# Second MLP layer as seven half-block products, interleaved with quarters of the next step's first layer

## The chip, the cores and the metric

One core of a Trainium2 chip runs the program. The metric is device time in microseconds of one launch; the time before is the median of three runs. A profiled execution of the same program gives the trace from which single instructions are read. Engines are named as in the profile: PE is TensorE (matmuls, with PEld for its weight loads), DVE is VectorE, ACT is ScalarE, POOL is GpSimd, SP is the queue that issues the DMAs.

## What is computed

A spectral block followed by an MLP, each with a layer norm ahead of it and a residual. The input has 2048 rows of 576 elements, the MLP has 4608 hidden elements, all in float32.

```python
def _A_ref(x, w_r, w_i):
    B, S, D = x.shape
    X = jnp.fft.rfft2(x, axes=(-2, -1))
    X = X * (w_r + 1j * w_i)
    return jnp.fft.irfft2(X, s=(S, D), axes=(-2, -1))

def _B_ref(x, w1, w2):
    h = jnp.einsum("bsd,df->bsf", x, w1)
    h = jnp.maximum(h, 0)
    return jnp.einsum("bsf,fd->bsd", h, w2)

h = x + _A_ref(_layernorm(x), A_w_r, A_w_i)
h2 = h + _B_ref(_layernorm(h), B_w1, B_w2)
```

The change lies in the MLP's second product, relu(h) times w2.

## The kernel before

The spectral block is done by matrix products with constant DFT matrices. Its inverse part runs in a loop over 16 row tiles and hands the normalised, transposed rows to the MLP (`project`) in four chunks `xc[c]` of 512 rows. The residual stays in `xs`, 16 tiles of 128 rows by 576, to which every partial result of the MLP is added.

The MLP is cut into 18 groups `g` of 256 hidden elements and 4 chunks `c` of 512 rows, so there are 72 steps, listed in `steps`: the first eight in an order of their own, partly woven into the inverse part, then group by group. The engines take their work in the order in which the code writes it (a manual schedule); the program sets the semaphores.

To get float32 accuracy out of the faster fp32r matmuls, every operand is held as a rounded part and a remainder (`h` and `l`), and each product is three matmuls: h by h, h by l, l by h. ACT writes the rounded part and DVE subtracts it from the original for the remainder. `split_weights` does this for a group's weights, part 0 for w1 and part 1 for w2 (L313).

A step has two halves. `mm1(i, a)` computes 128 hidden elements of a chunk (a is 0 or 1) as 14 matmuls with 512 columns into half of a PSUM tile of two banks; after the second half ACT takes the relu (L464) and DVE the remainder (L465). `mm2(i, tt)` multiplies one row tile of the chunk with the group's w2 in 12 matmuls of 288 columns, and DVE adds the PSUM tile to `xs` (L482). A step has four `mm2`. In the last loop, step i + 1's two `mm1` stand ahead of step i's four `mm2`, so that the relu runs beside matmuls that don't need it. The next group's weights are loaded five steps ahead and split three steps ahead. GpSimd (POOL) has no work in this loop. PSUM tiles come from a ring of four, and SBUF tiles of the tag "e" from ten buffers. In the last group each finished chunk of `xs` (in the last chunk: each finished tile) is stored by two DMAs.

Of the kernel before, what the change touches and what calls it, by code (L numbers as in the profile page):

```python
# [126 lines left out]
def kernel(ctx: ExitStack, tc: tile.TileContext, x, w_r, w_i, w1, w2, cc2, c1, fb, ib, c3, out):  # L127
    nc = tc.nc
# [15 lines left out]

    def mm(o, l, r, start, stop):
        nc.tensor.matmul(o, l, r, start=start, stop=stop)  # L146

    def act(o, i, **kw):
        nc.scalar.activation(o, i, AF.Copy, **kw)  # L149
# [142 lines left out]
    raw, wts = {}, {}  # L292

    def load_weights(g):
        v1, v2 = ebuf([128, 5, 256]), ebuf([128, 2, D])
        f = slice(256 * g, 256 * g + 256)
        nc.sync.dma_start(v1[:, 0:4], w1[0:512, f].rearrange("(a p) f -> p a f", p=128))
        for h in range(2):
            nc.sync.dma_start(v1[64 * h:64 * h + 64, 4], w1[512:576, f])
        nc.sync.dma_start(v2, w2[f, :].rearrange("(a p) d -> p a d", p=128))  # L300
        raw[g] = (v1, v2)

    def split_weights(g, part, eng):
        if g not in wts:
            if g % 2:
                w = tail[0][:, 4608:]
                w = (w[:, 0:1280], w[:, 1280:2560], w[:, 2560:3712], w[:, 3712:4864])
            else:
                w = (ebuf([128, 1280], F32R), ebuf([128, 1280], F32R), ebuf([128, 1152], F32R), ebuf([128, 1152], F32R))
            wts[g] = [v.rearrange("p (a n) -> p a n", a=a) for v, a in zip(w, (5, 5, 2, 2))]  # L310
        h, l = wts[g][2 * part:2 * part + 2]
        act(h, raw[g][part])
        eng.tensor_sub(l, raw[g][part], h)  # L313
# [63 lines left out]
    xs = sb([128, NT, D], "A")  # L377
# [7 lines left out]
    xc = [xc01[:, 0], xc01[:, 1], xc2]  # L385
    Es = {}

    def inv_d(t):
        pd = ps()
        ut = [dims(U, 64 * (32 * b + 2 * t), [1, 128]) for b in range(5)]  # L390
        for r in range(2):
            o = pd[:, 512 * r:512 * r + 290]
            mm(o, ut[4], lpv[:, r], True, False)
            for h in range(2):
                mm(o[:, 145 * h:145 * h + 145], ut[2 * ((r + h) % 2) + r], dev[:, 2 * r + h], False, h == 1)
        ez = ebuf([128, 578 + D])
# [7 lines left out]
        nc.vector.tensor_add(ea, ea, pb_)  # L404
        y = ez[:, 578:]
        nc.gpsimd.tensor_sub(dims(ez, 578 + 575, [-1, 287]), e0[:, 1:288], e1[:, 1:288])
        nc.vector.tensor_add(y[:, 0:289], e0, e1)  # L407
# [37 lines left out]
    hid = {}  # L445
    pend = {}

    def mm1(i, a):
        g, c = steps[i]
        w1h, w1l = wts[g][:2]  # L450
        if a == 0:
            pend[i] = ps()
        p = pend[i][:, 512 * a:512 * a + 512]
        f = slice(128 * a, 128 * a + 128)
        ops = []
        for kt in range(4):
            ops += [(w1h, kt, kt), (w1h, kt, 5 + kt), (w1l, kt, kt)]
        ops += [(w1h, 4, 4), (w1l, 4, 4)]
        for n_, (w, kt, xk) in enumerate(ops):
            mm(p, w[:, kt, f], xc[c][:, xk, :], n_ == 0, n_ == len(ops) - 1)  # L460
        if a == GF - 1:
            p = pend.pop(i).rearrange("p (a s) -> p a s", a=GF)
            hh, hl = sb([128, GF, 512], "D", 4, F32R), sb([128, GF, 512], "D", 4, F32R)
            nc.scalar.activation(hh, p, AF.Relu)  # L464
            nc.vector.scalar_tensor_tensor(hl, p, 0.0, hh, op0=ALU.max, op1=ALU.subtract)  # L465
            hid[i] = (hh, hl)
# [2 lines left out]

    def mm2(i, tt):  # L470
        g, c = steps[i]
        w2h, w2l = wts[g][2:]
# [9 lines left out]
        nc.vector.tensor_add(xt, xt, pv)  # L482
        if tt == CH - 1:
            seen[c] += 1
            hid.pop(i)
        if g == NG - 1 and (c == NC - 1 or tt == CH - 1):
            a = t if c == NC - 1 else CH * c
            for j in range(2):
                nc.sync.dma_start(ov[j, :, a:t + 1, :], xs[64 * j:64 * j + 64, a:t + 1, :])
# [71 lines left out]
```

## Time and profile before

| | |
|---|---|
| Time, median of 3 runs (lowest to highest) | 1108.53 us (1108.38 to 1109.08) |
| Profiled execution: its time | 1108.31 us |
| Profiled execution: span of its instructions | 1106.5 us |
| Granted TensorE clock, mean | 0.999 |
| HBM read, written | 42.23 MB, 4.72 MB |
| DVE additions to `xs` (L482): count, busy | 288, 216.4 us |
| Hidden relu on ACT (L464): count, busy | 72, 73.9 us |
| Relu remainder on DVE (L465): count, busy | 72, 88.2 us |

A row of the groups reads: line, engine, operation, tile written and tiles read by the program's names (buffer numbers left out), shapes, count, then the busy time in us and the mean duration of one in ns, then the engine's idle time just before them and what ended it. A row of the timeline reads: start in us from the start of the span, length in us, engine, line, operation, tiles, count, and in brackets the idle time before it. In the names, d is PSUM, D holds the hidden rows, X, B and C the normalised input chunks (X also split weights), e the small buffers, A is `xs`.

### The profile page before, as it was taken

To read this page: it belongs to the slowest core of one execution; us is meant where nothing else is said; L and a number is where in the kernel's file an instruction comes from. 1 tells how busy PE (TensorE), PEld (TensorE's weight loads), DVE (VectorE), ACT (ScalarE), POOL (GpSimd) and SP (SyncE) were. 2 spreads that over 40 slices of the span, in tenths; PEclk is the share of its full clock that TensorE was granted. 3 is DMA by queue.
4 is the path that set the end of the run, shared out by engine and by line. 5 is a ranking of instruction groups with operands and counts; after the bars stand their busy time and mean duration, and the time that the engine had idled before them with its cause. 6 is when DMAs were issued, how large, how long until landed. Compare 5 with 4: busy or idle time off the path is not lost.

```text
span 1106.5 us, 15686 instructions
## 1 busy us (share of the span) xinstructions
PE 1089.2 (98%) x6944; PEld 975.4 (88%) x6944; DVE 483.1 (44%) x739; ACT 199.3 (18%) x238; POOL 67.5 (6%) x116
## 2 busy tenths in 40 slices
PE   8999999999999999999999999999999999999997
PEld 7787778899899998989999899999889999998997
DVE  7577776434334343334343333434233434333333
ACT  4533253510101010101101011101010110101100
POOL 4200264300000000000000000000000000000000
PEclk9999999999999999999999999999999999999999
DMA  8922601111011001100200110011003001000015
GB/s 232 260 58 73 146 1 46 47 46 46 1 46 46 1 1 55 37 1 5 86 1 1 46 46 1 1 46 46 1 1 91 1 1 46 1 1 1 1 44 129
DMA packets 27573, 47.97 MB, mean 43 GB/s; under 512 B 2673, under 2 KB 18289, under 8 KB 27121
## 3 DMA queue, kind: packets, MB, share of 16 engines
q1 hardware_dynamic: 27504, 46.96, 15.6%
q8 instruction: 55, 0.90, 0.3%
q14 instruction: 14, 0.11, 0.0%
HBM read 42.23 MB, written 4.72 MB: 42 GB/s over the span
## 4 chain that ended last, share of the span: by engine, by line
PE 95%; DVE 3%; ACT 1%; issue 0%; POOL 0%; DMA 0%; SPq 0%; DVEq 0%; ACTq 0%; POOLq 0%
PE d L146 94%; PE d L434 1%; DVE st L206 0%; DVE A L416 0%; ACT e L220 0%; DMA X<-in_A_x_dram 0%; DVE e L313 0%; DVE e L404 0%; DVE e L403 0%; POOL r L210 0%; DVE e L407 0%; DVE e L348 0%; DVE e L250 0%; DVE e L347 0%; PE d L435 0%
## 5 line engine op out<-in xcount | busy, mean ns | idle before, releaser
L482 DVE TENSOR_TENSOR A<-A,d 128x576 f32<-128x576 f32 x288 | 216.4, 752 | 135.0 <-PE d L146 134.8
L465 DVE SCALAR_TENSOR_TENSOR D<-d,D 128x1024 fp32r<-128x1024 f32 x72 | 88.2, 1225 | 422.3 <-ACT D L464 422.3
L146 PEld LDWEIGHTS d<-e,D 128*128 128x128 f32 x1728 | 233.0, 188 | 3.9 <-DVE D L465 0.6
L146 PE MATMUL d<-e,D 128*128 128x288 f32 x1728 | 236.0, 295 | 0.3 <-DVE D L465 0.3
L146 PEld LDWEIGHTS d<-X,D 128*128 128x128 f32 x1728 | 232.2, 188 | 2.9
L146 PE MATMUL d<-X,D 128*128 128x288 f32 x1728 | 234.0, 294 | 0.0
L464 ACT ACTIVATE D<-d 128x1024 fp32r<-128x1024 f32 x72 | 73.9, 1027 | 767.4 <-PE d L146 767.4
L146 PE MATMUL d<-B,e 128*128 128x512 f32 x504 | 120.8, 395 | 0.4 <-DVE A L416 0.4
L146 PE MATMUL d<-B,X 128*128 128x512 f32 x504 | 119.0, 392 | 0.0
L146 PEld LDWEIGHTS d<-B,e 128*128 128x128 f32 x504 | 93.7, 188 | 21.6 <-ACT e L149 0.8
L146 PEld LDWEIGHTS d<-B,X 128*128 128x128 f32 x504 | 93.6, 188 | 19.4
L146 PE MATMUL d<-C,e 128*128 128x512 f32 x252 | 60.2, 395 | 0.0
L146 PE MATMUL d<-X,e 128*128 128x512 f32 x252 | 60.0, 394 | 0.0
L146 PE MATMUL d<-C,X 128*128 128x512 f32 x252 | 59.1, 391 | 0.0
L146 PE MATMUL d<-X 128*128 128x512 f32 x252 | 58.8, 390 | 0.0
L146 PEld LDWEIGHTS d<-X,e 128*128 128x128 f32 x252 | 46.8, 188 | 10.4
L146 PEld LDWEIGHTS d<-C,e 128*128 128x128 f32 x252 | 46.8, 188 | 10.3
L146 PEld LDWEIGHTS d<-C,X 128*128 128x128 f32 x252 | 46.8, 188 | 9.6
L146 PEld LDWEIGHTS d<-X 128*128 128x128 f32 x252 | 46.8, 188 | 9.3
L146 PE MATMUL d<-cc,e 128*128 128x256 f32 (+1 forms) x160 | 32.9, 361 | 3.0 <-DVE e L252 2.7
L146 PE MATMUL d<-e,A 128*64 128x145 f32 (+1 forms) x384 | 34.1, 327 | 0.8 <-ACT A L149 0.8
L146 PEld LDWEIGHTS d<-cc,e 128*128 128x128 f32 x160 | 28.5, 190 | 7.3 <-issue 2.9
(64 smaller groups left out, 629.3 us busy)
## 6 DMA issues: line engine op xcount, KB each, us to landing
e<-in_B_w_dram SPq DMA_DIRECT2D x18, 576.0 KB, 5.1
e<-in_B_w_dram SPq DMA_DIRECT2D x18, 512.0 KB, 3.7
A<-in_A_x_dram SPq DMA_DIRECT2D x16, 288.0 KB, 8.5
X<-in_A_x_dram SPq DMA_DIRECT2D x12, 288.0 KB, 7.4
out_dram<-A SPq DMA_DIRECT2D x6, 576.0 KB, 5.5
e<-in_B_w_dram SPq DMA_DIRECT2D x36, 64.0 KB, 3.6
B<-in_A_w_r_dram SPq DMA_DIRECT2D x15, 144.5 KB, 6.9
B<-in_A_w_i_dram SPq DMA_DIRECT2D x15, 144.5 KB, 7.0
```

The source lines that it names most:

```text
L146: nc.tensor.matmul(o, l, r, start=start, stop=stop)
L434: nc.tensor.transpose(pz[:, 128 * b:128 * b + 128], y[:, 128 * b:128 * b + 128], ident)
L464: nc.scalar.activation(hh, p, AF.Relu)
L465: nc.vector.scalar_tensor_tensor(hl, p, 0.0, hh, op0=ALU.max, op1=ALU.subtract)
L482: nc.vector.tensor_add(xt, xt, pv)
```

## The change

From step 8 on, the second layer of a step is computed by Strassen's scheme in Winograd's form. The hidden block is cut into four blocks: A11 and A21 are the two 256-row halves of the first 128 hidden elements, A12 and A22 those of the second. The group's w2 is cut into B11, B12, B21, B22 of 128 by 288. From these come the sums

- S1 = A21 + A22, S2 = S1 - A11, S3 = A11 - A21, S4 = A12 - S2 (on POOL, from relu copies p0 and p1 that ACT writes), and
- T1 = B12 - B11, T2 = B22 - T1, T3 = B22 - B12, T4 = B21 - T2 (on POOL, once a group, in `wino_sums`).

Seven products are made in place of eight: A11 B11, A12 B21, S2 T2, S1 T1, S3 T3, S4 B22, A22 T4. Each is 2 row tiles by 3 matmuls of 288 columns (`prod`, 42 matmuls a step where there were 48). Two PSUM tiles of two banks each, 0 and 1, collect them: a product with `first` false goes on top of what the tile holds, and DVE adds the tile to a quarter of the chunk (256 rows by 288 columns) after each product, seven additions in a step. Two further PSUM tiles take the first layer of the next step in turn.

The next step's two `mm1` are cut into quarters of 7 matmuls, which stand between the products: quarter 0, A11 B11, A12 B21, quarter 1, S2 T2, S1 T1, quarter 2, S3 T3, S4 B22, quarter 3, A22 T4. The relus, remainders and sums of the next step are written behind the quarter that completes them. The split of the weight blocks (`wino_w`) is spread over the last step of a group (`turn`) and the first of the next; that of w1 stays three steps ahead, which is the second step of a group. The stores of the last group are by quarter of a chunk. Steps 0 to 7 keep the old form; their split weights of group 1 partly lie in other buffers.

```diff
-    def split_weights(g, part, eng):
...
+    def split(h, l, v):
+        act(h, v)
+        nc.vector.tensor_sub(l, v, h)
...
-    def mm1(i, a):
+    def mm1(i, a, part=None):
...
-        if a == 0:
-            pend[i] = ps()
+        if a == 0 and not part:
+            pend[i] = wps[2 + i % 2] if i >= WINO else ps()
...
-            mm(p, w[:, kt, f], xc[c][:, xk, :], n_ == 0, n_ == len(ops) - 1)
+            if part is None or n_ // 7 == part:
+                mm(p, w[:, kt, f], xc[c][:, xk, :], n_ == 0, n_ == len(ops) - 1)
+        if i >= WINO:
+            return
...
+    WINO = 8
...
+    def wino_sums(g):
+        v = raw[g][1]
+        T = ebuf([128, 4, 288])
...
+        nc.gpsimd.tensor_sub(fs["T1"], fs["B12"], fs["B11"])
+        nc.gpsimd.tensor_sub(fs["T2"], fs["B22"], fs["T1"])
+        nc.gpsimd.tensor_sub(fs["T3"], fs["B22"], fs["B12"])
+        nc.gpsimd.tensor_sub(fs["T4"], fs["B21"], fs["T2"])
+
+    def wino_w(*names):
+        for n in names:
+            split(*wform(n), fs[n])
...
+    def relu_split(f, p):
+        h, l = f
+        nc.scalar.activation(h, p, AF.Relu)
+        nc.vector.scalar_tensor_tensor(l, p, 0.0, h, op0=ALU.max, op1=ALU.subtract)
+
+    def hid_a(i, k):
+        p = pend[i][:, 512 * k:512 * k + 512]
+        if k == 0:
+            relu_split(fs["A11"], p[:, :256])
+            nc.scalar.activation(fs["p0"], p.rearrange("p (a n) -> p a n", a=2), AF.Relu)
+            nc.gpsimd.tensor_sub(fs["S3"], fs["p0"][:, 0], fs["p0"][:, 1])
+        else:
+            relu_split(fs["A12"], p[:, :256])
+            nc.scalar.activation(fs["p1"], p.rearrange("p (a n) -> p a n", a=2), AF.Relu)
+            nc.gpsimd.tensor_add(fs["S1"], fs["p0"][:, 1], fs["p1"][:, 1])
+            nc.gpsimd.tensor_sub(fs["S2"], fs["S1"], fs["p0"][:, 0])
+            nc.gpsimd.tensor_sub(fs["S4"], fs["p1"][:, 0], fs["S2"])
+
+    def prod(i, a, b, bank, first, *to):
...
+        for tt in range(2):
+            q = slice(128 * tt, 128 * tt + 128)
+            for n_, (l, r) in enumerate(((ah, bh), (ah, bl), (al, bh))):
+                nc.tensor.matmul(P[:, tt], l[:, q], r, start=first and n_ == 0, stop=n_ == 2, skip_group_check=not first)
+        for hs, hd in to:
+            xt = xs[:, CH * c + 2 * hs:CH * c + 2 * hs + 2, 288 * hd:288 * hd + 288]
+            nc.vector.tensor_add(xt, xt, P)
...
+        quarter(0)
+        prod(i, "A11", "B11", 0, True, (0, 0))
+        if c == 0 and g > 2:
+            wino_w("T4")
+        prod(i, "A12", "B21", 1, True, (0, 0))
+        split(*fs["S12f"], fs["S12"])
+        if turn:
+            wino_w("B11", "B21")
+        if last:
+            store(c, 0, 0)
+        quarter(1)
+        prod(i, "S2f", "T2", 0, False, (0, 1))
+        split(*fs["S4f"], fs["S4"])
+        prod(i, "S1f", "T1", 1, True, (1, 1))
+        if turn:
+            wino_w("T2", "T1")
+        quarter(2)
+        prod(i, "S3f", "T3", 0, False, (1, 1))
...
+        if more:
+            split(*fs["S3f"], fs["S3"])
+        prod(i, "S4f", "B22", 1, False, (0, 1))
+        if turn:
+            wino_w("T3", "B22")
...
+        quarter(3)
+        prod(i, "A22", "T4", 0, False, (1, 0))
+        if more:
+            relu_split(fs["A22"], pend[i + 1][:, 768:1024])
...
         if i + 3 < len(steps) and steps[i + 3] == (steps[i + 3][0], 0):
-            for part in range(2):
-                split_weights(steps[i + 3][0], part, nc.vector)
-        if i + 1 < len(steps):
-            for a in range(GF):
-                mm1(i + 1, a)
+            split_weights(steps[i + 3][0], 0)
+            wino_sums(steps[i + 3][0])
...
+        if i >= WINO:
+            slot(i)
+            continue
```

The order of the instructions shows what this does to the engines that hand work to each other. On PE before, at the passage from a step's first layer to the last step's second (d_5502 the first layer's PSUM tile, d_5535 and d_5549 those of two row tiles, D_5436 and D_5437 the hidden rows and their remainders):

```order
L146 MATMUL d_5502<-B_1285,e_5310 128x512
L146 MATMUL d_5502<-B_1285,e_5311 128x512
L146 MATMUL d_5535<-X_1872,D_5436 128x288 x4
L146 MATMUL d_5535<-X_1872,D_5437 128x288 x2
L146 MATMUL d_5535<-X_1872,D_5436 128x288 x4
L146 MATMUL d_5535<-X_1872,D_5437 128x288 x2
L146 MATMUL d_5549<-X_1872,D_5436 128x288 x4
```

On PE after, from the last matmul of quarter 1 to the first of quarter 2 (d_394 the next step's first layer, d_392 and d_393 the two collecting tiles, D_385 the split S1 and S2), with the engines whose semaphores a matmul waits for in brackets:

```order
L146 MATMUL d_394_2681<-X_308_1872,e_436_6050 128x512
L549 MATMUL d_392_2679<-X_308_1872,D_385_2574 128x288 [waits DVE_49,Activation_49]
L549 MATMUL d_392_2679<-X_308_1872,D_385_2574 128x288
L549 MATMUL d_392_2679<-X_308_1872,D_385_2574 128x288 [waits DVE_49]
L549 MATMUL d_392_2679<-X_308_1872,D_385_2574 128x288 x3
L549 MATMUL d_393_2680<-X_308_1872,D_385_2574 128x288 x6
L146 MATMUL d_394_2681<-X_308_1872,e_435_6049 128x512 [waits Activation_49]
```

The products S2 T2 and S1 T1 stand between two quarters now. The first matmul of S2 T2 waits for S2's rounded part (ACT) and for the addition that empties d_392 (DVE), the third for the remainder (DVE). The first matmul of quarter 2 waits for ACT: by the semaphore's count that is the relu copy of the first half of d_394 (L532), although the quarter writes the other half.

On DVE before, around the split of a group's weights (additions from the d tiles, then w1 and w2, then the relu remainder and the next addition):

```order
L482 TENSOR_TENSOR A_1268<-A_1268,d_3444 128x576
L482 TENSOR_TENSOR A_1268<-A_1268,d_3458 128x576
L313 TENSOR_TENSOR X_1872<-e_3288,X_1872 128x1280
L313 TENSOR_TENSOR X_1872<-e_3289,X_1872 128x1152
L465 SCALAR_TENSOR_TENSOR D_3506<-d_3476,D_3505 128x1024
L482 TENSOR_TENSOR A_1268<-A_1268,d_3509 128x576
```

On DVE after, at the same place, the start of a group's second step (D_384 the remainder of A22, e_426 that of w1, d_392 and d_393 the products A11 B11 and A12 B21, D_385 the remainders of S1 and S2, D_383 that of the next A11):

```order
L526 SCALAR_TENSOR_TENSOR D_384_2573<-d_382_2571,D_384_2573 128x256 [waits Activation_49]
L305 TENSOR_TENSOR e_426_5232<-e_423_5021,e_425_5231 128x1280 [waits DMAHW6_49,DMAHW7_49,DMAHW5_49,Activation_49]
L552 TENSOR_TENSOR A_199_1268<-A_199_1268,d_392_2679 128x2x288 [waits PE_49]
L552 TENSOR_TENSOR A_199_1268<-A_199_1268,d_393_2680 128x2x288 [waits DVE_49,PE_49]
L305 TENSOR_TENSOR D_385_2574<-e_387_2576,D_385_2574 128x512 [waits Activation_49]
L526 SCALAR_TENSOR_TENSOR D_383_2572<-d_382_2571,D_383_2572 128x256 [waits Activation_49]
```

The split of w1 stands ahead of the two additions and of the split of S1 and S2, which the third matmul of S2 T2 waits for in the same step.

More of the change, by code (lines that the diff above doesn't have):

```diff
@@ L301, in load_weights, with split_weights @@
         raw[g] = (v1, v2)
-    def split_weights(g, part, eng):
[L304 to L313, printed above, removed]
+    def split(h, l, v):
+        act(h, v)
+        nc.vector.tensor_sub(l, v, h)
+    def split_weights(g, part):
+        if g == 1 and part == 0:
+            h, l = tail[0][:, 4608:5888], tail[0][:, 5888:7168]
+        else:
+            h, l = (ebuf([128, (1280, 1152)[part]], F32R) for _ in range(2))
+        h, l = (v.rearrange("p (a n) -> p a n", a=(5, 2)[part]) for v in (h, l))
+        wts[g, part] = h, l
+        split(h, l, raw[g][part])
     tail = []
@@ L446 @@
     pend = {}
-    def mm1(i, a):
+    def mm1(i, a, part=None):
         g, c = steps[i]
-        w1h, w1l = wts[g][:2]
-        if a == 0:
-            pend[i] = ps()
+        w1h, w1l = wts[g, 0]
+        if a == 0 and not part:
+            pend[i] = wps[2 + i % 2] if i >= WINO else ps()
         p = pend[i][:, 512 * a:512 * a + 512]
@@ L471, in mm2 @@
         g, c = steps[i]
-        w2h, w2l = wts[g][2:]
+        w2h, w2l = wts[g, 1]
         hh, hl = hid[i]
@@ L485, in mm2, with wform @@
             hid.pop(i)
-        if g == NG - 1 and (c == NC - 1 or tt == CH - 1):
-            a = t if c == NC - 1 else CH * c
-            for j in range(2):
-                nc.sync.dma_start(ov[j, :, a:t + 1, :], xs[64 * j:64 * j + 64, a:t + 1, :])
+    WINO = 8
+    wps, fs = [], {}
+    NAMES = ("B22", "T4", "B11", "B21", "T2", "T1", "T3")
+    def wform(n):
+        o = 6208 + 576 * NAMES.index(n)
+        return tail[0][:, o:o + 288], tail[0][:, o + 288:o + 576]
+    def wino_sums(g):
+        v = raw[g][1]
+        T = ebuf([128, 4, 288])
+        fs["T1"], fs["T2"], fs["T3"], fs["T4"] = (T[:, i] for i in range(4))
+        fs["B11"], fs["B12"], fs["B21"], fs["B22"] = v[:, 0, :288], v[:, 0, 288:], v[:, 1, :288], v[:, 1, 288:]
+        nc.gpsimd.tensor_sub(fs["T1"], fs["B12"], fs["B11"])
+        nc.gpsimd.tensor_sub(fs["T2"], fs["B22"], fs["T1"])
+        nc.gpsimd.tensor_sub(fs["T3"], fs["B22"], fs["B12"])
+        nc.gpsimd.tensor_sub(fs["T4"], fs["B21"], fs["T2"])
@@ new lines, in wino_w, with wino_tiles @@
+    def wino_w(*names):
+        for n in names:
+            split(*wform(n), fs[n])
+    def wino_tiles():
+        D1, D2, D3 = (sb([128, 4, 256], "D", 4, F32R) for _ in range(3))
+        E1, E2 = ebuf([128, 4, 256]), ebuf([128, 4, 256])
+        hs = tail[0][:, 5184:5696], tail[0][:, 5696:6208]
+        fs.update(p0=E1[:, 0:2], p1=E1[:, 2:4], S1=E2[:, 0], S2=E2[:, 1], S3=E2[:, 2], S4=E2[:, 3], S12=E2[:, 0:2])
+        fs.update(A11=(D1[:, 0], D1[:, 1]), A12=(D1[:, 2], D1[:, 3]), A22=(D2[:, 0], D2[:, 1]), S4f=(D2[:, 2], D2[:, 3]))
+        fs.update(S12f=(D3[:, 0:2], D3[:, 2:4]), S1f=(D3[:, 0], D3[:, 2]), S2f=(D3[:, 1], D3[:, 3]))
+        fs.update(S3f=(tail[0][:, 5696:5952], tail[0][:, 5952:6208]))
@@ new lines, in relu_split @@
+    def relu_split(f, p):
[8 more added lines that the diff above has]
+            nc.gpsimd.tensor_sub(fs["S3"], fs["p0"][:, 0], fs["p0"][:, 1])
+        else:
+            relu_split(fs["A12"], p[:, :256])
[3 more added lines that the diff above has]
+            nc.gpsimd.tensor_sub(fs["S4"], fs["p1"][:, 0], fs["S2"])
@@ new lines, in prod @@
+    def prod(i, a, b, bank, first, *to):
+        c = steps[i][1]
+        ah, al = fs[a]
+        bh, bl = wform(b)
+        P = wps[bank].rearrange("p (a n) -> p a n", a=2)[:, :, :288]
+        for tt in range(2):
[5 more added lines that the diff above has]
+            nc.vector.tensor_add(xt, xt, P)
@@ new lines, in store, with slot, quarter @@
+    def store(c, hs, hd):
+        if steps[-1][0] == NG - 1:
+            for j in range(2):
+                t, d = CH * c + 2 * hs, slice(288 * hd, 288 * hd + 288)
+                nc.sync.dma_start(ov[j, :, t:t + 2, d], xs[64 * j:64 * j + 64, t:t + 2, d])
+    def slot(i):
+        g, c = steps[i]
+        more, last, turn = i + 1 < len(steps), g == NG - 1, c == NC - 1 and g < NG - 1
+        def quarter(k):
+            if more:
+                mm1(i + 1, k // 2, k % 2)
+                if k % 2:
+                    hid_a(i + 1, k // 2)
+        quarter(0)
[16 more added lines that the diff above has]
+        prod(i, "S3f", "T3", 0, False, (1, 1))
+        if last:
+            store(c, 1, 1)
+        if more:
[3 more added lines that the diff above has]
+            wino_w("T3", "B22")
+        if last:
+            store(c, 0, 1)
+        quarter(3)
+        prod(i, "A22", "T4", 0, False, (1, 0))
+        if more:
+            relu_split(fs["A22"], pend[i + 1][:, 768:1024])
+        if last:
+            store(c, 1, 0)
@@ L506 @@
             load_weights(1)
-            tail.append(sb([128, 9472], "X", dt=F32R))
+            tail.append(sb([128, 10240], "X", dt=F32R))
             xc.append(tail[0][:, :4608].rearrange("p (a n) -> p a n", a=9))
@@ L522 @@
         if t in (2, 4):
-            split_weights(0, t // 2 - 1, nc.vector)
+            split_weights(0, t // 2 - 1)
         if t in (18, 19):
-            split_weights(1, t - 18, nc.vector)
+            split_weights(1, t - 18)
         if gen:
@@ L531 @@
         if i + 3 < len(steps) and steps[i + 3] == (steps[i + 3][0], 0):
-            for part in range(2):
-                split_weights(steps[i + 3][0], part, nc.vector)
-        if i + 1 < len(steps):
-            for a in range(GF):
-                mm1(i + 1, a)
+            split_weights(steps[i + 3][0], 0)
+            wino_sums(steps[i + 3][0])
+        if i == WINO - 2:
+            wino_w("B11", "B21", "T2", "T1", "T3")
+        if i == WINO - 1:
+            wps += [None, None, ps(), None]
+            wino_tiles()
+        if i == WINO:
+            wps[:2] = ps(), ps()
+            wps[3] = ps()
+        if i >= WINO:
+            slot(i)
+            continue
+        for a in range(GF):
+            mm1(i + 1, a)
+            if i == WINO - 1:
+                hid_a(i + 1, a)
         for tt in range(CH):
             mm2(i, tt)
+        if i == WINO - 1:
+            relu_split(fs["A22"], pend[i + 1][:, 768:1024])
+            split(*fs["S3f"], fs["S3"])
+            wino_w("B22", "T4")
 _INS = ["A_x", "A_w_r", "A_w_i", "B_w1", "B_w2"]
```

## The prediction

> **What bounds the kernel now.** I read the page first: engine shares, the granted clock, and the chain that ended last.
>
> ```profile
> span 1106.5 us, 15686 instructions
> PE 1089.2 (98%) x6944; PEld 975.4 (88%) x6944; DVE 483.1 (44%) x739; ACT 199.3 (18%) x238; POOL 67.5 (6%) x116
> ...
> PEclk9999999999999999999999999999999999999999
> ...
> PE 95%; DVE 3%; ACT 1%; issue 0%; POOL 0%; DMA 0%; SPq 0%; DVEq 0%; ACTq 0%; POOLq 0%
> ```
>
> TensorE is at full clock and makes 95% of the chain. The chain in order of time says where:
>
> ```profile
> 223.12 876.66 PE d L146 x5216
> 1099.81 0.75 DVE A L482
> ```
>
> From 223 us to the end there is one unbroken run of matmuls: nothing is waited for, so the time is a count of matmuls times their spacing. The spacing comes from TensorE's timeline in the middle of the run:
>
> ```profile
> 702.86 6.56 PE L146 MATMUL d<-e,D 128*128 128x288 f32 x48
> 709.25 6.59 PE L146 MATMUL d<-C,e 128*128 128x512 f32 x28
> 715.68 6.56 PE L146 MATMUL d<-e,D 128*128 128x288 f32 x48
> ```
>
> From start to start, the 48 matmuls of the second layer take 709.25 - 702.86 = 6.39 us (0.133 each), the 28 of the first 715.68 - 709.25 = 6.43 us (0.230 each). A step is 12.82 us. A change pays here only if it takes matmuls out, and only as long as TensorE still never waits.
>
> **What is removed.** In steps 8 to 71 the second layer has 7 products of 6 matmuls, 42 in place of 48, of the same shape (128x288). That is 6 x 0.133 = 0.80 us a step, 64 x 0.80 = **51.1 us**. The first layer's 28 stay. All of this lies on the chain.
>
> **What is added** must fit beside a step of 12.02 us. Prices from the groups by shape, in the window 700 to 800 us and (last four rows) over the whole run:
>
> ```profile
> L482 DVE TENSOR_TENSOR A<-A,d 128x576 f32<-128x576 f32 x32 | 24.1, 752 | 15.3 <-PE d L146 15.3
> L465 DVE SCALAR_TENSOR_TENSOR D<-d,D 128x1024 fp32r<-128x1024 f32 x8 | 9.8, 1225 | 48.6 <-ACT D L464 48.6
> L149 ACT ACTIVATE e<-e 128x1280 fp32r<-128x1280 f32 x1 | 1.3, 1265 | 0.0
> L313 DVE TENSOR_TENSOR e<-e,e 128x1280 fp32r<-128x1280 f32 x1 | 1.5, 1486 | 0.0
> ...
> L149 ACT ACTIVATE e<-d 128x512 f32<-128x512 f32 x16 | 9.5, 594 | 0.0
> L149 ACT ACTIVATE e<-d 128x290 f32<-128x290 f32 x16 | 6.6, 411 | 13.0 <-PE d L146 9.6 <-POOL e L406 1.5 <-DVE e L407 1.5
> L406 POOL TENSOR_TENSOR e<-e 128x287 f32<-128x287 f32 x16 | 14.7, 918 | 96.0 <-DVE e L404 96.0
> L442 POOL TENSOR_TENSOR B<-e,B 128x512 fp32r<-128x512 f32 x8 | 10.2, 1272 | 9.4 <-ACT e L149 9.4
> ```
>
> VectorE's rows at 576, 1024 and 1280 lie on one line, 0.15 us plus 1.04 ns an element: 256 elements cost 0.42, 288 0.45, 512 0.69. ScalarE's at 290 and 512 give 0.38 for 256. A normal step then has on VectorE 7 additions of 576 (5.3), three relu remainders of 256 (1.3), splits of 512, 256 and 256 (1.5): 8.1 us of 12.0; the last step of a group adds 6 splits of 288 (2.7), the second one the first-layer split (1.5). ScalarE has about 3.7. Neither is the bound by its sum, so the question is order. How fast work is handed over:
>
> ```profile
> 703.06 1.03 ACT L464 ACTIVATE D<-d 128x1024 fp32r<-128x1024 f32 x1 [11.73 <-PE d L146]
> ...
> 704.12 1.23 DVE L465 SCALAR_TENSOR_TENSOR D<-d,D 128x1024 fp32r<-128x1024 f32 x1 [6.72 <-ACT D L464]
> 705.26 0.74 DVE L482 TENSOR_TENSOR A<-A,d 128x576 f32<-128x576 f32 x1
> ```
>
> TensorE's last matmul of the first layer gives way at 702.86 and ScalarE starts 0.20 later; ScalarE to VectorE is 0.03; two VectorE operations that wait for nothing overlap by 0.09. VectorE to ScalarE I take at 0.02, and a waiting TensorE resumes like this:
>
> ```profile
> 119.78 0.46 DVE L407 TENSOR_TENSOR e<-e 128x289 f32<-128x289 f32 x1
> ...
> 120.26 0.41 ACT L149 ACTIVATE e<-d 128x290 f32<-128x290 f32 x1 [1.49 <-DVE e L407]
> ...
> 190.85 1.22 DVE L465 SCALAR_TENSOR_TENSOR D<-d,D 128x1024 fp32r<-128x1024 f32 x1 [1.70 <-ACT D L464]
> ...
> 192.13 2.90 PE L146 MATMUL d<-e,D 128*128 128x288 f32 x20 [0.33 <-DVE D L465]
> ...
> 194.87 0.60 PE L434 MATMUL d<-ident,e 128*128 128x128 f32 x4
> ```
>
> VectorE ends at 192.07 and TensorE restarts at 192.13; its 20 matmuls take 2.74 us to the next row where 20 x 0.133 is 2.66. So a wait ends 0.06 + 0.08 = 0.14 us after what it waited for.
>
> **Wait one: the third quarter of each step.** In the new order the first matmul of quarter 2 waits for ScalarE, for the copy of the first half of the hidden rows (L532), since both halves lie in one PSUM tile. That copy waits for VectorE's remainder, which waits for ScalarE's relu, which waits for quarter 1. The chain from the end of quarter 1 is 0.20 + 0.38 + 0.03 + 0.42 + 0.02 + 0.59 + 0.14 = 1.78 us. Beside it stand two products, 12 x 0.133 = 1.60. TensorE waits 0.18 us. In 48 of the 64 steps that is 8.6 us (the other 15 with a successor are covered by wait two). Bounds: 0 if each of the five handovers is 0.04 shorter, 0.4 a step (19 us) if each is that much longer; I take 8.6.
>
> **Wait two: the second step of each group.** There the split of the next group's first-layer weights stands ahead of the step's additions on VectorE. Time 0 is the end of quarter 3 before: remainder of A12 done at 1.03, copy at 1.64, relu of A22 at 1.93, ScalarE's half of the split at 3.11, VectorE's half at 4.63, then the additions of A11 (5.29) and A12 (6.07, it waits for the first), then the split of S1 and S2 at 6.67, plus 0.14. TensorE wants that remainder for the third matmul of S2 x T2, at 0.80 + 1.61 + 0.80 + 0.80 + 1.61 + 0.27 = 5.89. It waits 0.92 us, 15 times. In other steps the same chain has no 1.49 in it, and the split ends about 5.4, with some 0.3 us to spare.
>
> GpSimd makes this one uncertain. It has had nothing to do in this part, and now gets four operations of 256 elements a step and four of 288 a group. The trace shows what it does to VectorE's operations with two SBUF inputs, which all splits are:
>
> ```profile
> 119.92 0.87 POOL L406 TENSOR_TENSOR e<-e 128x287 f32<-128x287 f32 x1 [77.96 <-DVE e L404]
> ...
> 141.73 1.27 POOL L442 TENSOR_TENSOR B<-e,B 128x512 fp32r<-128x512 f32 x1
> 142.00 1.32 DVE L407 TENSOR_TENSOR e<-e 128x289 f32<-128x289 f32 x1
> ```
>
> L407 takes 0.46 when it starts first; started behind L442 it takes 1.32 and ends 0.32 after it. Whoever comes second waits: L406, started 0.14 into an L407, had 0.32 of its 0.87 beside it, which leaves 0.55. So 256 elements on GpSimd cost between 0.49 (that 0.55, scaled) and 0.82 (the whole L406 row, scaled); I take 0.7, nearest to half of L442 (0.64). Then S1, S2 and S4 run from 1.7 to about 4.0, and VectorE's half of the weight split wants to start at 3.14, within 0.1 us of S4's start. If S4 is first, 0.7 is added to the wait. I take 1.2 us, between 0.92 and 1.6: 15 x 1.2 = 18 us, bounds 14 and 25.
>
> The Trainium skill has this as a rule, SBUF — State Buffer, Who interferes with whom: a VectorE instruction with two SBUF inputs contends with GpSimd reads, and the pair of ports is an exclusive lock. The rows of L407 agree; without the rule the term would be 14, with it up to 25.
>
> **Ends.** Entering: both first-layer halves of step 8 stand back to back, so the 1.78 us chain is exposed once: 1.8. Last step: there is no first layer between the products, so each product that comes back to a PSUM accumulator waits for its addition (0.20 + 0.75 + 0.14 = 1.1 the first time, less later) and S1 and S2 for their split; I take 3, bounds 2 and 5. Output: today the stores pile up behind the last additions.
>
> ```profile
> 1097.62 6.19 SPq L489 DMA_DIRECT2D out_dram<-A  x7
> ```
>
> The queue still issues until 1103.81, 3.2 us behind the last addition's end at 1100.56. Afterwards a last pair of stores of the same size remains, about 1.2 us of issue: -2, bounds 0 and -3. Weight loads stay 18 pairs, issued two steps ahead of their split; they cost nothing as long as that lead (some 24 us) covers a landing, and a late one would stop the split of wait two.
>
> **Sum**, against the profiled execution's 1108.31 (span 1106.5; the median of the runs is 1108.53): -51.1 + 8.6 + 18 + 1.8 + 3 - 2 = -21.7, so **1087 us**. With the bounds of the terms 1072 to 1108; the likeliest case's own range is 1078 to 1100.
>
> **Rivals.**
> *TensorE stays dense.* If the handovers are shorter than I read them and VectorE finds room, both waits vanish: 1108.3 - 51.1 + 1.8 + 3 - 2 = 1060; one of them alone gone gives 1069 or 1078. For it: wait one is only 0.18 us, a tenth of its chain. Against it: wait two is five times that, and every duration in it has a row. 0.22 for 1060 to 1078.
> *The lock falls on every step: slower.* The split of S1 and S2 has 0.3 us to spare in a normal step. If GpSimd's operations take L442's 1.27 in full and hold that split once a step, TensorE waits about 0.9 us in each of 48 steps and about 2.2 in the 15, 43 + 33 = 76, so 1108.3 - 51.1 + 76 + 3 = 1136. It turns the change into a loss from about 0.8 us of wait a step, that is from a GpSimd operation of about 1.1 us. Against it: L406 less its blocked time is 0.55. 0.16.
> *No gain, because products are not fewer.* The new order has 42 matmuls at L549 a step; this is out.
> *Waits that just eat the gain*, 1100 to 1110: 0.10, of which 0.06 within 0.2% (2 us, about what a measurement of this kernel can tell from no change).
>
> The forecast has 0.52. Faster by over 0.2%: 0.52 + 0.22 + 0.04 = 0.78; same 0.06; slower 0.16. The range that leaves out about 0.1 of each end is 1064 to 1112.
>
> **What would show it.** TensorE's timeline should have gaps of about 0.2 us ahead of the third quarter, released by ScalarE's L532, and gaps of about 1 us after the second matmul of S2 x T2 in every fourth step, released by VectorE's L305. Two matmuls of the new product should still be 0.133 apart. GpSimd's 256-element rows should be 0.5 to 0.8; L305 of 1280 above 1.49 means the lock. Wrong would be: a gap after every step's S2 x T2 (the lock in all steps), no gaps at all, or a spacing of the products other than 0.133.

## The result, and the profile after

The changed kernel takes 1098.07 us (median of 4 runs, 1096.92 to 1098.96) against 1108.8 for the kernel before beside it (1108.38 to 1110.37): ratio 0.99, 95% interval 0.9883 to 0.9917. That is 10.7 us less, where 21.7 less were forecast. The profiled execution took 1097.28 us, 11.0 below the profiled one of before. The page after, in the parts that were read before (span, busy time by engine, granted clock, the chain that ended last by engine), and the group of VectorE's additions:

```profile
span 1095.2 us, 17045 instructions
PE 1061.8 (97%) x6560; PEld 927.7 (85%) x6560; DVE 743.2 (68%) x1347; ACT 386.4 (35%) x782; POOL 333.6 (30%) x436
...
PEclk9999999999999999999999999999999999999999
...
PE 84%; DVE 8%; ACT 3%; DMA 2%; issue 1%; POOL 0%; SPq 0%; ACTq 0%; DVEq 0%; POOLq 0%
...
L552 DVE TENSOR_TENSOR A<-A,d 128x576 f32<-128x576 f32 x448 | 335.6, 749 | 112.5 <-PE d L549 107.3
```

384 matmuls are gone (6944 to 6560), the clock is as before, and VectorE, which had 3% of the chain, has 8%: TensorE now waits. For what, the list of waits says (waiting engine and line, releaser, us in total, times, longest):

```profile
PEld d L549 <- DVE D L305: 17.2, 17, 1.1
...
PEld d L146 <- ACT e L532: 14.0, 49, 2.0
...
PE d L549 <- DVE D L305: 13.2, 16, 0.9
```

The counts are those of the two forecast waits: 15 second steps of a group and two in the last step for VectorE's L305, 48 steps and the entry for ScalarE's L532. TensorE's timeline of the second step of a group and of a normal step, in the middle of the run (start, length, engine, line, count):

```profile
699.95 0.96 PE L549 MATMUL d<-X 128*128 128x288 f32 x6
...
705.57 1.75 PE L549 MATMUL d<-X,D 128*128 128x288 f32 x12
707.15 1.79 PE L146 MATMUL d<-C,e 128*128 128x512 f32 x7
708.78 0.44 PE L549 MATMUL d<-X,D 128*128 128x288 f32 x2
710.09 1.59 PE L549 MATMUL d<-X,D 128*128 128x288 f32 x10 [0.87 <-DVE D L305]
711.52 1.78 PE L146 MATMUL d<-C,e 128*128 128x512 f32 x7
713.13 0.96 PE L549 MATMUL d<-X 128*128 128x288 f32 x6
...
721.97 1.75 PE L549 MATMUL d<-X,D 128*128 128x288 f32 x12
723.76 1.89 PE L146 MATMUL d<-X,e 128*128 128x512 f32 x7
725.49 0.96 PE L549 MATMUL d<-X 128*128 128x288 f32 x6
...
737.85 0.95 PE L549 MATMUL d<-X 128*128 128x288 f32 x6
```

The rows of six with X alone on the input are S3 T3, once a step. From one to the next is 13.18 us over the group's second step (699.95 to 713.13) and 12.36 over normal ones (to 725.49, to 737.85). Over the run the mean of the 15 is 13.17 and that of 47 normal ones 12.37. The matmuls alone would need 12.80 - 6 x 0.1323 = 12.01 (before's mean step, taken over its whole unbroken run, less six matmuls at its mean spacing). In a normal step the loss stands at two rows: S2 T2 and S1 T1 take 1.79 from start to start (721.97 to 723.76) where the twelve of A11 and A12 take 1.58 (705.57 to 707.15), and quarter 2 takes 1.73 (723.76 to 725.49) where quarter 1 takes 1.63 (707.15 to 708.78). In the group's second step it is one gap, from the second matmul of S2 T2 to its third.

The terms, as forecast and as the trace has them:

| term | forecast, us | measured, us | from |
|---|---|---|---|
| matmuls saved | -51.1 | -50.8 | 384 x 0.1323 |
| wait one, 48 normal steps | +8.6 | +17.5 | 12.37 - 12.01 |
| wait two, 15 group steps | +18 | +17.4 | 13.17 - 12.01 |
| entry | +1.8 | +2.4 | TensorE's starts; 0.36 of it ahead of 223 us |
| last step | +3 | +3.15 | its five gaps on TensorE, 1.02 + 0.68 + 0.83 + 0.32 + 0.30 |
| output behind it | -2 | -1.1 | last addition's end to the span's, 4.84 for 5.94 |
| sum | -21.7 | -11.5 | measured -11.0 |

The terms are sums over steps, and not all of a step's loss is waiting: the experiments below leave 12.08 us a step when both waits are gone, 0.07 above the 12.01 that the matmuls alone would need. Of the 17.5 and the 17.4 some 3 and 1 are this.

So 9 of the 11 us that are missing lie in the 48 normal steps, where wait one stands: 5 in the wait itself, 3 in those 0.07. The wait's chain, in the timeline of the same normal step (releasers in brackets):

```profile
722.23 0.39 ACT L525 ACTIVATE D<-d 128x256 fp32r<-128x256 f32 x1 [1.85 <-PE d L146]
...
722.65 0.42 DVE L526 SCALAR_TENSOR_TENSOR D<-d,D 128x256 fp32r<-128x256 f32 x1 [0.69 <-ACT D L525]
...
723.11 0.60 ACT L532 ACTIVATE e<-d 128x512 f32<-128x512 f32 x1 [0.49 <-DVE D L526]
...
723.76 1.46 PEld L146 LDWEIGHTS d<-X,e 128*128 128x128 f32 x7 [0.27 <-ACT e L532]
```

Quarter 1 gives way at 721.97 (S2 T2 starts). Then 0.26 to ScalarE, relu 0.39, 0.03, remainder 0.42, 0.04, copy 0.60, 0.05 to TensorE's weight load: 1.79, and about 0.10 more that quarter 2 is slow. 1.89 against 1.78 forecast.

### The profile page after: what moved, and what is told of

Its sections match the earlier page's. It is cut to its first block, busy times and chain, and to the rows that moved or that the text cites. A ratio compares the mean times of both kernels' runs of the same rounds, so it can differ in the third digit from the quotient of the medians.

```text
span 1095.2 us, 17045 instructions
## 1 busy us (share of the span) xinstructions
PE 1061.8 (97%) x6560; PEld 927.7 (85%) x6560; DVE 743.2 (68%) x1347; ACT 386.4 (35%) x782; POOL 333.6 (30%) x436
## 4 chain that ended last, share of the span: by engine, by line
PE 84%; DVE 8%; ACT 3%; DMA 2%; issue 1%; POOL 0%; SPq 0%; ACTq 0%; DVEq 0%; POOLq 0%
PE d L146 54%; PE d L549 29%; DVE A L552 2%; DVE e L305 2%; ACT e L149 2%; DMA A<-in_A_x_dram 1%; ACT D L525 1%; DVE D L305 1%; DVE D L526 1%; PE d L435 1%; DVE st L206 0%; DVE A L417 0%; ACT e L220 0%; DMA X<-in_A_x_dram 0%; SPq L157 0%
## 5 line engine op out<-in xcount | busy, mean ns | idle before, releaser
L552 DVE TENSOR_TENSOR A<-A,d 128x576 f32<-128x576 f32 x448 | 335.6, 749 | 112.5 <-PE d L549 107.3
L549 PE MATMUL d<-X,D 128*128 128x288 f32 x2304 | 352.2, 296 | 14.5 <-DVE D L305 13.2
L549 PEld LDWEIGHTS d<-X,D 128*128 128x128 f32 x2304 | 330.1, 188 | 37.2 <-DVE D L305 17.2
L146 PE MATMUL d<-B,e 128*128 128x512 f32 x952 | 246.3, 399 | 2.5 <-ACT e L532 1.6
L146 PEld LDWEIGHTS d<-B,e 128*128 128x128 f32 x952 | 171.0, 188 | 41.4 <-ACT e L532 9.4
L537 POOL TENSOR_TENSOR e<-e 128x256 f32<-128x256 f32 x64 | 47.5, 743 | 367.7 <-ACT e L536 367.7
L526 DVE SCALAR_TENSOR_TENSOR D<-d,D 128x256 fp32r<-128x256 f32 x192 | 81.5, 424 | 105.7 <-ACT D L525 105.7
L533 POOL TENSOR_TENSOR e<-e 128x256 f32<-128x256 f32 x64 | 50.0, 781 | 195.7 <-ACT e L532 195.7
L305 DVE TENSOR_TENSOR D<-e,D 128x512 fp32r<-128x512 f32 (+1 forms) x128 | 94.5, 738 | 14.1 <-ACT D L149 14.1
L305 DVE TENSOR_TENSOR X<-e,X 128x288 fp32r<-128x288 f32 (+2 forms) x177 | 74.6, 445 | 0.9 <-ACT X L149 0.9
L146 PE MATMUL d<-e,D 128*128 128x288 f32 x384 | 53.6, 297 | 0.3 <-DVE D L469 0.3
L146 PEld LDWEIGHTS d<-e,D 128*128 128x128 f32 x384 | 52.0, 188 | 1.5 <-DVE D L469 0.6
```

Of the source, the lines that this page charges most:

```text
L305: nc.vector.tensor_sub(l, v, h)
L526: nc.vector.scalar_tensor_tensor(l, p, 0.0, h, op0=ALU.max, op1=ALU.subtract)
L533: nc.gpsimd.tensor_sub(fs["S3"], fs["p0"][:, 0], fs["p0"][:, 1])
L537: nc.gpsimd.tensor_add(fs["S1"], fs["p0"][:, 1], fs["p1"][:, 1])
L549: nc.tensor.matmul(P[:, tt], l[:, q], r, start=first and n_ == 0, stop=n_ == 2, skip_group_check=not first)
L552: nc.vector.tensor_add(xt, xt, P)
```

## The experiments

Two theories stood after this reading. **Mine:** the 17.5 is the chain relu, remainder, copy, longer than its cover; the 17.4 is the order of VectorE's queue, w1's split ahead of S1's and S2's. **The rivals:** GpSimd's new work takes the port from VectorE and delays these chains (it would then also hold them when the order is better), or the matmuls of the new order are simply dearer than those of the old.

**The copy first.** A11 is then split from the copy in SBUF instead of from PSUM, so PSUM is read once and the copy waits for nothing but quarter 1.

```diff
     def hid_a(i, k):
         if k == 0:
-            relu_split(fs["A11"], p[:, :256])
             nc.scalar.activation(fs["p0"], p.rearrange("p (a n) -> p a n", a=2), AF.Relu)
+            split(*fs["A11"], fs["p0"][:, 0])
```

> The first half of the next hidden block is read from PSUM once only: ScalarE's relu copy p0 comes first, and A11's two parts are made from p0 in SBUF. Theory of the two waits: quarter 2 waits for a chain of 0.26 + 0.60 + 0.05 us in place of 1.8, which the two products (1.6 us) cover, so the gap of 0.20 us and the restart of 0.10 go in 48 steps (-14), and entering step 8 costs 0.9 less: about 1083 us. Rival (VectorE is so full that a wait removed comes back at the next product): TensorE has gaps in front of S2 T2 or S4 B22 in normal steps, and the time stays within 4 us of 1098. Rival (the quarters and products are slower by themselves): the same, with no gaps.

Measured: 1082.82 us (1080.99 to 1083.02), ratio to before 0.9759 (0.9745 to 0.9774). ScalarE's and TensorE's timeline in a normal step:

```profile
714.87 1.75 PE L549 MATMUL d<-X,D 128*128 128x288 f32 x12
715.12 0.60 ACT L531 ACTIVATE e<-d 128x512 f32<-128x512 f32 x1 [1.92 <-PE d L146]
716.46 1.77 PE L146 MATMUL d<-X,e 128*128 128x512 f32 x7
718.07 0.95 PE L549 MATMUL d<-X 128*128 128x288 f32 x6
```

The copy ends at 715.72, 0.74 ahead of quarter 2. The two products take 1.59 and quarter 2 takes 1.61: both pieces of the loss are gone, and normal steps take 12.04 to 12.12 (one 12.29), 12.08 in the mean. The group's second step still takes 13.11. Wait one is that chain. What comes back is 12.37 - 12.08 = 0.29 in each of 48 steps, 14 us, and about 1 at the entry; the other 0.07 a step of the table's 17.5 stays.

**The order alone.** Copy ahead of A11's relu, both still from PSUM; nothing else.

```diff
         if k == 0:
-            relu_split(fs["A11"], p[:, :256])
             nc.scalar.activation(fs["p0"], p.rearrange("p (a n) -> p a n", a=2), AF.Relu)
+            relu_split(fs["A11"], p[:, :256])
```

> The changed kernel with one thing turned round: the relu copy p0 stands ahead of A11's relu, both still read PSUM. Quarter 2 then waits for VectorE's remainder of A11 (L526) instead of ScalarE's copy. Theory (the gap is the length of this chain less two products): 0.25 + 0.60 + 0.29 + 0.03 + 0.42 + 0.15 = 1.74 us in place of 1.89, against 1.60, so the loss in a normal step falls from 0.30 to about 0.14 us, 48 x 0.16 = 8 us: about 1090 us, with the gap's releaser changed from ScalarE to VectorE. Rival (it is ScalarE's load, not the chain): the same work is done, so the time stays at 1098.

Measured: 1090.56 us (1090.48 to 1090.63), ratio 0.9827 (0.981 to 0.9843).

```profile
719.04 1.75 PE L549 MATMUL d<-X,D 128*128 128x288 f32 x12
719.30 0.60 ACT L531 ACTIVATE e<-d 128x512 f32<-128x512 f32 x1 [1.92 <-PE d L146]
719.80 0.38 ACT L525 ACTIVATE D<-d 128x256 fp32r<-128x256 f32 x1
720.21 0.43 DVE L526 SCALAR_TENSOR_TENSOR D<-d,D 128x256 fp32r<-128x256 f32 x1 [1.17 <-ACT D L525]
720.69 1.90 PE L146 MATMUL d<-X,e 128*128 128x512 f32 x7
```

That is about half of what the copy first gained. The copy is done at 719.90, yet quarter 2 starts at 720.69, 0.05 behind the remainder's end at 720.64 (0.05 to 0.07 in the normal steps of the trace): it waits for the last reader of the PSUM tile, whichever that is. The chain is shorter (ScalarE's two operations overlap by 0.10, and one hand-over is gone), but the cover of 1.59 is still short of it, and the two products' stretch takes 1.65. Quarter 2 writes the other 512 columns, which neither operation reads; the wait goes by the whole tile. The Trainium skill, PSUM — Partial Sum Buffer, PSUM bank collisions raise a hardware error, asks to guard by bank and quadrant. By the same page of the Trainium skill, Specifications (TRN2), a bank holds 512 fp32 values. By these two, two tiles of 512 columns would need no such wait; no run here tried it.

**w1's split later.** On VectorE behind S1 T1's addition instead of ahead of the step; the weight sums stay.

```diff
@@ slot, behind prod(i, "S1f", "T1", ...) and its wino_w
+        if i + 3 < len(steps) and steps[i + 3] == (steps[i + 3][0], 0):
+            split_weights(steps[i + 3][0], 0)
         quarter(2)
@@ main loop
-            split_weights(steps[i + 3][0], 0)
+            if i < WINO:
+                split_weights(steps[i + 3][0], 0)
             wino_sums(steps[i + 3][0])
```

> The split of the next group's w1 is written behind S1 T1 of the same step, the sums T1 to T4 on GpSimd stay where they are. Theory of the two waits: the 1.05 us gap in S2 T2 of 15 steps goes; these steps become like the others (12.36 in place of 13.17): -12, about 1086 us. Rival (GpSimd's lock does it): T1 to T4 now start right behind S4 and hold VectorE's split of S1 and S2 for up to one operation of 0.8 us, so 0.3 to 0.8 us of the gap stays in each of the 15 steps, 1090 to 1096 us.

Measured: 1085.58 us (1084.22 to 1085.65), ratio 0.9785 (0.9771 to 0.98). The same stretch, VectorE's split among TensorE's rows:

```profile
703.51 1.75 PE L549 MATMUL d<-X,D 128*128 128x288 f32 x12
705.30 1.87 PE L146 MATMUL d<-C,e 128*128 128x512 f32 x7
...
706.74 1.49 DVE L305 TENSOR_TENSOR e<-e,e 128x1280 fp32r<-128x1280 f32 x1
707.00 0.96 PE L549 MATMUL d<-X 128*128 128x288 f32 x6
```

S2 T2 and S1 T1 run as one piece of twelve; steps now take 12.36 in the mean (12.31 to 12.41, one 12.70), wait one included. Wait two was the place of one 1.5 us operation in VectorE's queue.

**The weight sums later too.** GpSimd's T1 to T4 (four operations of 288) join the split behind S1 T1, off the step's busy beginning. If GpSimd's port were the cost, this would gain more.

```diff
+            split_weights(steps[i + 3][0], 0)
+            wino_sums(steps[i + 3][0])
...
```

> As the run before, with T1 to T4 moved behind S1 T1 as well. Two waits: about 1086 us, as the run before. Lock rival: faster than the run before by 4 to 10 us, since no GpSimd operation lies beside the split of S1 and S2 in any step.

Measured: 1086.39 us (1086.0 to 1086.55), ratio 0.9795 (0.978 to 0.9809): nothing gained. The port rival loses its main prediction. The port does bind, as the changed kernel's own rows at the group's second step show:

```profile
706.37 1.54 DVE L305 TENSOR_TENSOR e<-e,e 128x1280 fp32r<-128x1280 f32 x1 [0.73 <-ACT e L149]
706.63 1.88 POOL L539 TENSOR_TENSOR e<-e,e 128x256 f32<-128x256 f32 x1
...
709.35 0.68 DVE L305 TENSOR_TENSOR D<-e,D 128x512 fp32r<-128x512 f32 x1
```

S4 on GpSimd, started behind the split, takes 1.88 (1.87 or 1.88 in all 15 such steps) where it takes 0.74 in the others: it waits out the rest of the split. That is the rule of the Trainium skill, SBUF — State Buffer, Who interferes with whom, by which the shared pair of ports is an exclusive lock, and the trace agrees with it. But VectorE came first in this row (1.54, where the group by shape of before has 1.49), and S4 is wanted only at S4 B22. That product starts 0.80 behind S3 T3 (713.13 to 713.93), as in a normal step (725.49 to 726.29), so the lock costs TensorE nothing here. In every normal step the port binds the other way too: the remainder of S4 on VectorE, beside GpSimd's next operation, takes 0.76, where the remainders of 256 from PSUM take 0.42. The split of S1 and S2, which TensorE waits for, is not held in any step (0.68 to 0.69).

**Both cures together**, the copy first and the later split with its sums (the diffs of the first and of the fourth kernel), run twice.

> Both edits: p0 first, and w1's split with T1 to T4 behind S1 T1. Two waits: 12.36 and 13.17 us a step become about 12.05, -15 in normal steps, -17 in the 15 others, -1 at the entry: about 1065 us. Rival (VectorE too full): gaps come back elsewhere in the steps that split weights, 1075 us or more.

> The kernel with both edits again, beside g1 on the same chip: 1066 to 1067 us; it says whether g1's 1 to 2 us are a difference.

Measured: 1066.58 us (1065.45 to 1067.34), ratio 0.9613 (0.9597 to 0.9629), and 1066.39 (1065.32 to 1067.47), ratio 0.9604 (0.9588 to 0.962). Steps take 12.03 to 12.17 (one 12.30), 12.08 in the mean, and the page's chain says that TensorE is the bound again:

```profile
PE 94%; DVE 2%; DMA 2%; ACT 1%; issue 0%; POOL 0%; SPq 0%; DVEq 0%; ACTq 0%; POOLq 0%
```

The two gains more than add (15.3 and 11.7 alone, 31.5 together): a group's second step meets wait one as soon as wait two is gone from it. With the later split alone it falls to 12.36, with both cures to 12.08, and 15 x 0.28 = 4.2 of the 4.5 that the sum of the two leaves out.

**Eight products.** Is the gain really the number of matmuls? This kernel is the one with both cures, and A11 B11's six matmuls are made twice into the same sums.

```diff
-        for tt in range(2):
+        for tt in (0, 1, 0, 1)[:4 if a == "A11" else 2]:
```

> The kernel with both edits, and in each step from 8 on the 6 matmuls of A11 B11 are made a second time (start flag set again, same sums), so that a step has 48 matmuls of 288 columns as before the change. Theory (the gain is matmuls times spacing): +6 x 0.132 x 64 = 51 us, 1066.6 + 51 = 1117 us, that is some 9 us more than the kernel before. Rival (part of the gain comes from the interleaving or the smaller tiles): clearly less than +51.

Measured: 1117.51 us (1116.41 to 1118.45), ratio 1.0069 (1.0054 to 1.0084). TensorE's row of A11, A11 again and A12:

```profile
701.97 2.54 PE L549 MATMUL d<-X,D 128*128 128x288 f32 x18
```

50.9 us over the kernel with both cures, 0.133 for each of 384 matmuls. So the products' matmuls cost in the new order what they did in the old. What the new form costs of itself, with 48 such matmuls a step as before, is 0.0069 x 1108.5 = 7.6 us (6 to 9): a step is 12.88 in the mean where before's is 12.80, 5 us over the run; the rest is left to the ends, and was not priced term by term.

**GpSimd doubled.** To price a slower GpSimd, S1, S2 and S4 are each computed twice on GpSimd, in the kernel with both cures. S2, and with it the split of S1 and S2, then comes two operations later.

```diff
             nc.gpsimd.tensor_add(fs["S1"], fs["p0"][:, 1], fs["p1"][:, 1])
+            nc.gpsimd.tensor_add(fs["S1"], fs["p0"][:, 1], fs["p1"][:, 1])
...
```

> The kernel with both edits, and S1, S2 and S4 are each computed twice on GpSimd (the same sums), 0.75 us an operation. This prices the rival in which GpSimd decides. Theory: the chain to S2 grows by 2 x 0.75 us; it has some 0.9 us to spare on ScalarE and VectorE, so S2 T2 waits about 0.6 us in every step with a successor: 63 x 0.6 = 38 us, about 1105 us. Rival (there is room for it): 1068 us or less. Rival (the lock adds to it, VectorE's splits are held too): over 1112 us.

Measured: 1109.67 us (1107.11 to 1110.11, 10 runs), ratio 0.9995 (0.9986 to 1.0004).

```profile
712.74 0.74 POOL L540 TENSOR_TENSOR e<-e,e 128x256 f32<-128x256 f32 x1
...
713.51 0.63 ACT L149 ACTIVATE D<-e 128x512 fp32r<-128x512 f32 x1 [3.03 <-POOL e L540]
...
714.18 0.69 DVE L305 TENSOR_TENSOR D<-e,D 128x512 fp32r<-128x512 f32 x1 [0.58 <-ACT D L149]
...
714.21 0.53 PE L552 MATMUL d<-X,D 128*128 128x288 f32 x2
...
714.92 1.58 PE L552 MATMUL d<-X,D 128*128 128x288 f32 x10 [0.19 <-DVE D L305]
```

S2's rounded part is ready at 714.14, just in time for S2 T2 in this row; its remainder is late: from 714.21 the third matmul is due at 714.48 and starts at 714.92, and S2 T2 and S1 T1 take about 2.15 instead of 1.59. The list of waits has this wait 63 times. The kernel with both cures, undoubled, has at this place:

```profile
715.28 0.63 ACT L149 ACTIVATE D<-e 128x512 fp32r<-128x512 f32 x1 [1.40 <-POOL e L538]
...
716.87 0.68 DVE L305 TENSOR_TENSOR D<-e,D 128x512 fp32r<-128x512 f32 x1
```

The rounded part is ready at 715.91, and VectorE comes to the remainder only at 716.87, behind its additions: 0.96 of slack. Two operations of 0.74 more are 1.5; 1.5 - 0.96 = 0.5, close to the loss of 0.56 a step. One step in four takes 0.35 more still (13.00, the others 12.65), and the whole gain is gone. These 15 x 0.35 = 5 us are what the time lies above the 1105 expected; where in these steps they arise was not followed up. So a longer chain on GpSimd does reach TensorE in every step, with 0.96 us of slack before it does. It is not the lock of the prediction's slower rival: the split of S1 and S2 takes 0.69 here as elsewhere, it only starts later.

**A miss: the copy first for the other half too.** By the same argument A12 is split from p1. T4's weight split moves behind that of S1 and S2.

```diff
         else:
-            relu_split(fs["A12"], p[:, :256])
             nc.scalar.activation(fs["p1"], p.rearrange("p (a n) -> p a n", a=2), AF.Relu)
+            split(*fs["A12"], fs["p1"][:, 0])
...
```

> The kernel with both edits; A12 is made from p1 in SBUF too, and T4's split stands behind the split of S1 and S2. Theory: S1 and S2 start 0.8 us sooner, T4's 0.45 us no longer lies ahead of their split in the first step of a group (0.07 us each now): -1 from 15 steps, and 0.3 to 0.8 in the last step: about 1065 us. Rival (more operations with two SBUF inputs meet GpSimd): slower than 1066.6.

Measured: 1085.04 us (1084.09 to 1086.01), ratio 0.9777 (0.9762 to 0.9791), 18.5 us slower than with both cures. In the list of waits an entry of 2 times (1.4 us, with both cures) has become one of 64, and the timeline shows its reason:

```profile
PEld d L549 <- DVE A L552: 31.2, 64, 1.9
```

```profile
710.14 1.80 PE L146 MATMUL d<-X,e 128*128 128x512 f32 x7
710.23 0.74 POOL L537 TENSOR_TENSOR e<-e 128x256 f32<-128x256 f32 x1 [0.67 <-ACT e L535]
710.63 0.61 DVE L305 TENSOR_TENSOR D<-e,D 128x256 fp32r<-128x256 f32 x1 [1.08 <-ACT D L149]
711.17 0.74 DVE L552 TENSOR_TENSOR A<-A,d 128x576 f32<-128x576 f32 x1
711.96 1.86 PE L549 MATMUL d<-X,D 128*128 128x288 f32 x12
```

A12's split now waits for the copy and, having two SBUF inputs, runs beside GpSimd's S1 (0.61 instead of 0.42). Behind it in VectorE's queue stands the addition of A22 T4, whose matmuls gave way to quarter 0 at 710.14; it starts 1.03 later and ends at 711.91. It empties the accumulator that the next A11 B11 writes, due at 710.14 + 1.63 = 711.77. TensorE starts at 711.96 and pays about 0.3 in 63 steps. The theory ahead of this run looked at what the copies wait for, and not at who stands behind them. Its rival named the lock, and the lock has a part: the 0.19 that the split takes longer is as much as the 0.19 that TensorE starts late.

**The same, with the addition first.** A12's split is put behind A22 T4's addition.

```diff
         else:
             nc.scalar.activation(fs["p1"], p.rearrange("p (a n) -> p a n", a=2), AF.Relu)
-            split(*fs["A12"], fs["p1"][:, 0])
...
         prod(i, "A22", "T4", 0, False, (1, 0))
         if more:
+            split(*fs["A12"], fs["p1"][:, 0])
             relu_split(fs["A22"], pend[i + 1][:, 768:1024])
```

> As f3, with A12's split written behind the addition of A22 T4, so that VectorE empties accumulator 0 first. Theory (in f3 the addition stood behind A12's split, which waits for p1 and for GpSimd's S1, and A11 B11 waited for it): the 0.20 + 0.10 us gap behind quarter 0 goes in all 63 steps, 63 x 0.3 = 19, about 1065 us. Rival (splitting from SBUF is what slows f3, through the lock with GpSimd): the gap stays, about 1085 us.

Measured: 1064.51 us (1064.46 to 1066.45), ratio 0.9594 (0.958 to 0.9608).

```profile
710.54 0.75 DVE L551 TENSOR_TENSOR A<-A,d 128x576 f32<-128x576 f32 x1 [1.46 <-PE d L548]
711.21 0.42 DVE L305 TENSOR_TENSOR D<-e,D 128x256 fp32r<-128x256 f32 x1
711.54 0.42 DVE L526 SCALAR_TENSOR_TENSOR D<-d,D 128x256 fp32r<-128x256 f32 x1
```

The addition starts as soon as TensorE lets it (its releaser is PE) and ends at 711.29, ahead of A11 B11 at 711.97, and the 20 us are back. The exchange takes both away, the wait ahead of the addition and the lock's 0.19 in it, so the place in the queue is a cure for the whole of that miss; how much of it the lock made, these two runs don't separate. The port still binds behind the exchange, but on GpSimd's side, where S2 beside this split takes 0.99 instead of 0.74, and TensorE doesn't wait for it. Against both cures alone the ranges overlap, so the second split from SBUF itself gains nothing that these runs tell. Either version beats both kernels, by 40 us and more against before.

## Why the prediction was right in kind and off by half

- **What is removed**: right. 384 matmuls at 0.1323 are 50.8 us; the run with eight products gives 50.9.
- **Wait one**: right place (first matmul of quarter 2), right releaser (L532), right mechanism (taking the chain apart removed it, and only it); the term was mis-sized, 8.6 where the normal steps lose 17.5. The chain was put at 1.78 and is 1.89; against a cover of 1.59 that makes 0.30 a step in place of 0.18, or 14 us. Over half of the 0.11 is the first handover, read at 0.20 in before, where it is 0.26 after. The other 0.07 a step, 3 us here, is matmuls that stand a little wider than in before, most of it in the quarters (1.624 in the mean for 1.612); the prediction put that at nothing, and it stays when the wait is gone. Its cause was not tested. This term is the step that failed. The bounds given, 0 to 19, did hold it.
- **Wait two**: right, 17.4 against 18, and the later split removed it. But of that size 0.28 a step was set aside for a split held by GpSimd's S4, and S4 came second: the split lost 0.05. The rest came from a chain that ran 0.2 late (additions done 1.52 behind the split, forecast 1.44; restart). The term was right partly by luck.
- **Ends**: the entry was 0.6 dearer, the gain at the output 0.9 smaller, the last step as forecast. At the output the queue of the stores still issues until 1092.42 (1069.84 + 22.58), 2.1 behind the last addition, where 1.2 was forecast. For the entry the chain is exposed once:

```profile
274.55 3.41 PE L146 MATMUL d<-B,e 128*128 128x512 f32 x14
279.52 3.51 PE L146 MATMUL d<-B,e 128*128 128x512 f32 x14 [1.56 <-ACT e L532]
```

  From 274.55 the 14 matmuls fill 14 x 0.230 = 3.22, and the next starts at 279.52: 1.75 lost, as forecast (1.78). The rest of the 2.4 is spread, 0.36 of it before the first unbroken stretch; its cause stays open.
- **TensorE stays dense**, the faster rival, did not come in this kernel. With both cures the time is 1066 to 1067, in its 1060 to 1078, but because the order was changed: the handovers were longer than read, and not shorter as this rival had it.
- **The lock on every step**, the slower rival, did not come: GpSimd's row is 0.74, under the 1.1 put as its point, and the split of S1 and S2 is not held in any step. The lock does fall in every step, on the remainder of S4 (0.76 for 0.42), which has room. Doubling GpSimd's work, in the kernel with both cures, took the whole gain away, by a later S2 and not by the lock.

## What to carry to other kernels

A wait is a chain less its cover; when both are near 1.8 us, a tenth of a microsecond in the chain can nearly double the wait, and a term that recurs 48 times deserves bounds rather than a value. When a PSUM tile feeds several consumers, copy it out first with nothing ahead of the copy, and split from SBUF what isn't urgent. But each operation moved in an in-order queue must be judged by what stands behind it: here the addition that empties an accumulator had to go ahead of a split that waits for other engines (1064.51 us against 1085.04).

## What the runs showed of the hardware that was not expected

- The handover from TensorE to ScalarE varied between kernels: 0.20 in the kernel before, 0.25 to 0.26 in nearly all rows of the changed kernel, of the copy first, of the order alone and of both cures (714.87 to 715.12, 719.04 to 719.30), and 0.19 to 0.21 again in the two kernels where A12 is split from SBUF too. Why was not tested.
- A gap costs TensorE more than its own length: the seven matmuls of quarter 2 take 1.73 behind a wait and 1.61 without one, and the ten behind the group's gap 1.43 (710.09 to 711.52) where 10 x 0.1323 is 1.32.
- The lock of the port costs the one that comes second about the rest of the other's operation: S4, started 0.26 into a split of 1.54, takes 1.88 for 0.74. It still cost TensorE nothing there: S4 B22 is not late, and moving GpSimd's T1 to T4 away as well gained nothing (1086.39 against 1085.58).
